# Small products of the first attention blocks on VectorE, and query spreads at every second unit, in a fused forward and backward kernel

## The chip, the cores and the metric

One core of one Trainium2 chip runs the whole program in one launch. The metric is the device time of that launch in microseconds (us). For this kernel about 0.3% (2.7 us) can be told from no change.

## The reference: what is computed

A gated mix of two branches, forward and backward. `A` is a causal sliding-window attention (2048 tokens, width 512, 32 heads of 16, window 256), `B` is a gated feed-forward net (512 to 1376 to 512). The kernel returns the output and the gradients of seven inputs.

```python
def _A_ref(x, wqkv, wo):
    qkv = (x @ wqkv).reshape(B, S, 3, H, Dh)  # q, k, v per head
    scores = einsum("bhqd,bhkd->bhqk", q, k) * (Dh ** -0.5)
    mask = (idx[:, None] - idx[None, :] >= 0) & (idx[:, None] - idx[None, :] < W)
    p = softmax(where(mask, scores, -1e9))
    return einsum("bhqk,bhkd->bhqd", p, v).reshape(B, S, D) @ wo
def _B_ref(x, W_gate, W_up, W_down):
    gate = x @ W_gate
    return ((gate * (gate > 0)) * (x @ W_up)) @ W_down
g = sigmoid((x * gate_w).sum(-1, keepdims=True))
out = g * _A_ref(x, wqkv, wo) + (1 - g) * _B_ref(x, W_gate, W_up, W_down)
# returned: out and the vjp of out for x, wqkv, wo, W_gate, W_up, W_down, gate_w
```

## The kernel before

The program has three stages. The feed-forward stage runs to about 245 us of the profiled span. The attention stage, forward and backward together, runs from there to about 712 us; the change lies in it. A last stage multiplies by the output weights and finishes the gradient of x.

**Units.** The 32 heads stand in four head groups of eight (`c` = 0 to 3) and the 2048 tokens in 16 blocks of 128 (`j` = 0 to 15). For every head group and query block the kernel goes through the key blocks of the window, each in two halves of four heads. One such piece, four heads of one query block against one key block, is a unit; there are 360. In the first head group block 0 has units U0 and U1, block 1 U2 to U5, block 2 U6 to U11, block 3 U12 to U17, block 4 U18 to U23, and so on, six to a block. A unit has a role: `d` (diagonal key block), `m` (the one before) or `f` (two before).

**What a unit does.** TensorE makes the scores `ST` (line 697), ScalarE their exponentials into `Pu` (L706), GpSimd masks them if the role is d or f (`affine_select`, L708 and L711), TensorE makes `dPT`, the products of the output gradient with v (L720), VectorE multiplies `Pd = Pu * dPT` (L725, called `gradp`; the tiles are named PPd, PPm or Pd by role), and TensorE sums over the keys into `BA` (L734 and L736, called `rowsum`). `ST` and `dPT` share four PSUM buffers, so a new one waits for an old one's reader. After the last unit of a block ScalarE copies `BA` to `BAs` (L740). `BA` has one buffer and `BAs` two: the first rowsum of the next block waits for the copy, and the copy of a block waits until the block two before it no longer uses its `BAs`.

**Small products.** `small_ops` (L768) then works on one block's `BAs`. `dve` (L780) takes the reciprocal of the row sums on VectorE. Four pieces follow on GpSimd: `pool1` (L783, L784, L786: the row term `ndel` and two products into `rq`), `pool2` (L789 into `rq`, L791 the attention output into `rows_st`), `pool3` (L794 and L795, a product and a sum in place in `BAs`), and `pool4` (L798, the gradient of q into `rows_st`). `pool4` is the last to read `BAs`. Each product is 128 partitions by 128 elements, with f32 inputs from SBUF, or bf16 for the rows.

**The order of the work** is written out by hand. A loop runs over step `n`, and step n issues the front of unit n, the `gradp` of unit n-2 and the `rowsum` of unit n-4 (`LAG` = 4). Events of a step hang in `ev`: GpSimd's events are issued after the front of the step (its mask included), VectorE's after the step's gradp. Every engine works through its own instructions in the order of issue. With s = n-2 at a block's last rowsum, the reciprocal stands at step s+3 and the four pieces at s+4, s+5, s+6, s+7; for block 0 of every head group at s+5, s+6, s+9, s+10. So in the first head group block 0 (s = 3) has its pieces at steps 8, 9, 12 and 13, block 1 (s = 7) at 11 to 14, block 2 (s = 13) at 17 to 20, block 3 (s = 19) at 23 to 26.

**Query spreads.** While four blocks are worked on, the projections of the next four are fed in between (`project_parts`): Q, dO, a transpose by DMA, K, V, and a transpose of K and V. Q and dO of eight heads lie in one tile `zT`; four copies on VectorE (`spread`, L125, 32 partitions by 1024 elements each) take them apart into the sparse tile `z` that the next blocks' `ST` and `dPT` read. The four are set when dO has been issued, at steps n+1, n+2, n+3 and n+4. The copies of K and V (L174, L196, L197) on VectorE follow when their projections are issued. There are 15 sets of four; the first is issued at once with its dO, before the attention loop, the other 14 by steps.

Of the kernel before, what the change touches and what calls it, by code (L numbers as in the profile page):

```python
# [9 lines left out]
ALU = mybir.AluOpType  # L10
# [12 lines left out]
def kernel(  # L23
# [20 lines left out]
    nc = tc.nc  # L44
# [8 lines left out]
    Dh = D // H  # L53
# [24 lines left out]
    def bc(ap2, n):  # L78
        return ap2.unsqueeze(2).to_broadcast([ap2.shape[0], ap2.shape[1], n])
# [37 lines left out]
    if True:  # L117
# [5 lines left out]
        def spread(gi, k):  # L123
            rows = slice(32 * k, 32 * k + 32)
            nc.vector.tensor_copy(zt[gi % ZB][rows, :, k, :, :].rearrange("p w t q -> p w (t q)"),  # L125
                                  proj[groups[gi]]["z"][rows, :, :])
# [76 lines left out]
    with ExitStack() as p1, tc.manual_schedule():  # L203
# [148 lines left out]
        for fc in range(FC):  # L352
            for tg in range(NTG):
                k = Step()
# [170 lines left out]
    if True:  # L525
# [242 lines left out]
        def small_ops(c, j, s):  # L768
            rows = proj[(c, j // TPG)]["rows"]
            jl = j % TPG  # L770
            rows_st = sts[c]
            BAs = BAsb[(c, j)]
            hd = lambda a: a.rearrange("p (h d) -> p h d", h=HG)
            rinv = wk.tile([P, HG], F32, tag="rinv", name="rinv")
            ndel = wk.tile([P, HG], F32, tag="ndel", name="ndel")
            rq = wk.tile([P, HG, 3 * Dh], BF, tag="rq", bufs=4, name="rq")
            RQ[(c, j)] = rq

            def dve():
                nc.vector.reciprocal(rinv[:], BAs[:, :, 16])  # L780

            def pool1():
                nc.gpsimd.tensor_tensor(out=ndel[:], in0=BAs[:, :, 33], in1=rinv[:], op=ALU.mult)  # L783
                nc.gpsimd.tensor_tensor(out=rq[:, :, 2 * Dh:3 * Dh], in0=hd(rows[:, 0, jl, :]),  # L784
                                        in1=bc(rinv[:], Dh), op=ALU.mult)
                nc.gpsimd.tensor_tensor(out=rq[:, :, 0:Dh], in0=rq[:, :, 2 * Dh:3 * Dh], in1=bc(ndel[:], Dh), op=ALU.mult)  # L786

            def pool2():
                nc.gpsimd.tensor_tensor(out=rq[:, :, Dh:2 * Dh], in0=hd(rows[:, 1, jl, :]),  # L789
                                        in1=bc(rinv[:], Dh), op=ALU.mult)  # L790
                nc.gpsimd.tensor_tensor(out=hd(rows_st[:, j, 3, :]), in0=BAs[:, :, 17:33], in1=bc(rinv[:], Dh), op=ALU.mult)  # L791

            def pool3():
                nc.gpsimd.tensor_tensor(out=BAs[:, :, 0:16], in0=BAs[:, :, 0:16], in1=bc(ndel[:], Dh), op=ALU.mult)  # L794
                nc.gpsimd.tensor_tensor(out=BAs[:, :, 0:16], in0=BAs[:, :, 0:16], in1=BAs[:, :, 34:50], op=ALU.add)  # L795

            def pool4():
                nc.gpsimd.tensor_tensor(out=hd(rows_st[:, j, 0, :]), in0=BAs[:, :, 0:16], in1=bc(rinv[:], Dh), op=ALU.mult)  # L798

            if c == DC - 1 and j > 8:  # L800
                return ((s + 3, "dve", dve), (s + 3, "pool+", pool1), (s + 4, "pool", pool2), (s + 6, "pool", pool3), (s + 7, "pool", pool4))
            at = (5, 6, 9, 10) if j == 0 else (4, 5, 6, 7)
            return ((s + 3, "dve", dve),) + tuple((s + a, "pool", f) for a, f in zip(at, (pool1, pool2, pool3, pool4)))

        GT = min(2, NT)
# [46 lines left out]
        with tc.manual_schedule():  # L852
            ev = {}
# [6 lines left out]
            n = 0  # L860
# [15 lines left out]
            def background():  # L876
                f, more = bgq.pop(0)
                store = f()
                if store is not None:
                    copies.append(store)  # L880
                    if len(copies) > 2 or gi + 2 >= len(groups):
                        ev.setdefault(n + 2, []).append(("dma", flush))
                return more
# [15 lines left out]
            while n <= NU + LAG or ev or cdq or bgq:  # L899
                now = ev.pop(n, [])  # L900
                u = units[n] if n < NU else None
                if u is not None:
                    gi = u.c * NTG + u.j // TPG
# [37 lines left out]
                if w is not None:  # L941
                    rowsum(w)
                    if not w.dma:
                        flip(w)
                    if w.last:
                        for s, eng, f in small_ops(w.c, w.j, n - 2):
                            ev.setdefault(s, []).append((eng, f))
                        done = [w.j - 2] if w.j >= 2 else []
                        if w.j == NT - 1:
                            done += [NT - 2, NT - 1]  # L950
                        for kb in done:
                            qbs = range(kb, min(NT, kb + 3))
                            for qb in qbs:
                                for half in range(2):
                                    e = n + (1 if qb < w.j else 5)
                                    cdq.append((e, w.c, kb, qb, half, qb == qbs[-1] and half == 1))
# [8 lines left out]
                if n >= NU:  # L965
                    if bgq:
                        held = background()
                    elif n > NU + 1:
                        for _ in range(2):
                            if len(S2["grads"]) > DC:  # L970
                                S2["grads"].pop(0)()
                elif held and credit > 0.3:
                    held = background()
                    credit -= 0.65
                elif prq and not held and ((credit > 0.4 and n > fed + 1) or due - n <= len(prq)):
                    fed = n
                    credit -= (0.44, 0.86, 0.86, 0.1, 0.86, 0.86)[len(prq) - 1]
                    prq.pop(0)()
                    if len(prq) == 4:
                        for k in range(NP):  # L980
                            ev.setdefault(n + 1 + k, []).append(("dve", lambda gi=gi, k=k: spread(gi + 1, k)))
                        ev.setdefault(n + 1, []).append(("dma", flush))
                    if not prq:
                        late += plan.get(gi + 1, [])
                elif bgq and len(prq) <= 2 and credit > 0.3:
                    held = background()
                    credit -= 0.65
# [28 lines left out]
    with ExitStack() as p56:  # L1016
        x_r5 = x_r

        with ExitStack() as p6, tc.manual_schedule():
# [43 lines left out]
            for g in range(NG):  # L1063
# [5 lines left out]
                for tl in range(GT):  # L1069
# [14 lines left out]
                    for c in range(DC):  # L1084
# [16 lines left out]
                                            op=ALU.mult)  # L1101
# [72 lines left out]
```

## Time and profile before

| | us |
|---|---|
| median of three runs | 902.75 (902.62, 902.75, 905.12) |
| the profiled execution | 903.0 |
| its span on the core | 901.3 |

The profiled execution lies 0.25 us above the median. Its span is 1.7 us shorter than its time. The granted TensorE clock was 1.0. VectorE was busy 511.1 us (57%), ScalarE 446.0 (49%), GpSimd 492.5 (55%). "Idle before" in a row of the timeline is the time for which the engine had nothing to run before the instruction, and the name behind the arrow is what ended it. A matmul's duration in a row is modelled and longer than the time after which the next one starts.

### The profile page before, as it was taken

The numbers are of one execution on the slowest core, as the hardware profiler recorded it, in microseconds if no ns is written. First come the engines' busy times: TensorE is split into PE (matmuls) and PEld (weight loads), VectorE is DVE, ScalarE is ACT, GpSimd is POOL, SyncE is SP. The second block draws the span as 40 slices with busy tenths as digits, with TensorE's granted clock in tenths as the row PEclk, the third lists the DMA queues.
The fourth block names the chain that finished last, engine by engine and source line by source line (L and its number), as shares of the span: only waits on it lengthen the run. The fifth ranks groups of instructions, "written<-read, shape, count | busy, mean of one in ns | idle before, by whom it ended". The sixth has DMA issues, their size and how long they took to land.

```text
span 901.3 us, 25949 instructions
## 1 busy us (share of the span) xinstructions
PE 889.4 (99%) x10607; PEld 560.3 (62%) x10607; DVE 511.1 (57%) x946; ACT 446.0 (49%) x787; POOL 492.5 (55%) x937
## 2 busy tenths in 40 slices
PE   9999999999999999999999999999999999999998
PEld 5555655655657777677776677766677544444445
DVE  4533334334468887678886788876787101333343
ACT  6422232222368778667776677766787112111111
POOL 4644545545277778667778567876788100222232
PEclk9999999999999999999999999999999999999999
DMA  9988989999999999998999989999999998998940
GB/s 299 204 182 195 197 178 209 214 230 201 202 144 159 196 183 190 194 169 153 175 187 179 190 162 176 192 193 184 209 190 195 225 259 219 252 277 234 198 125 30
DMA packets 520983, 174.57 MB, mean 194 GB/s; under 512 B 446816, under 2 KB 519744, under 8 KB 520864
## 3 DMA queue, kind: packets, MB, share of 16 engines
q1 hardware_dynamic: 498624, 150.62, 90.5%
q10 hardware_dynamic: 20608, 17.70, 7.0%
q0 software_dynamic: 1632, 4.59, 1.5%
q8 instruction: 83, 1.36, 0.6%
q14 instruction: 36, 0.29, 0.1%
HBM read 34.37 MB, written 36.24 MB: 78 GB/s over the span
## 4 chain that ended last, share of the span: by engine, by line
PE 87%; DVE 3%; SPq 3%; DMA 3%; ACT 2%; POOL 1%; issue 1%; DVEq 0%; POOLq 0%; ACTq 0%
PE wps L420 8%; PE ST L697 8%; PE dPT L720 8%; PE dxps L1076 7%; PE pt L763 5%; PE wps L651 5%; PE dhps L367 4%; PE CD L551 4%; PE BA L734 4%; PE ups L367 4%; PE gps L367 4%; PE pp L138 4%; PE dxps L1106 4%; PE dps L423 4%; PE bps L1051 3%; PE CD L554 3%
## 5 line engine op out<-in xcount | busy, mean ns | idle before, releaser
L697 PE MATMUL ST<-z,K 128*128 128x512 bf16 x360 | 136.0, 378 | 2.0 <-DVE PPm L725 1.2
L720 PE MATMUL dPT<-z,V 128*128 128x512 bf16 x360 | 135.9, 378 | 1.1 <-DVE Pd L725 0.5
L708 POOL TENSOR_SCALAR_AFFINE_SELECT PPd<-PPd 128x512 bf16<-128x512 bf16 x128 | 81.3, 636 | 77.9 <-ACT PPd L706 77.9
L381 POOL TENSOR_TENSOR hT<-rg,upm 128x512 bf16<-128x512 bf16 x44 | 51.0, 1159 | 113.1 <-DVE upm L379 98.5
L420 PE MATMUL wps<-dgu_r,x_r 128*128 128x256 bf16 (+1 forms) x704 | 101.8, 270 | 0.2 <-DVE wst L74 0.2
L725 DVE TENSOR_TENSOR PPd<-PPd,dPT 128x512 bf16<-128x512 bf16 x128 | 87.0, 680 | 19.3 <-PE dPT L720 12.6
L711 POOL TENSOR_SCALAR_AFFINE_SELECT Pu<-Pu 128x512 bf16<-128x512 bf16 x112 | 72.0, 643 | 34.9 <-ACT Pu L706 33.8
L706 ACT ACTIVATE PPd<-ST 128x512 bf16<-128x512 f32 x128 | 77.0, 603 | 23.8 <-PE ST L697 18.9
L725 DVE TENSOR_TENSOR Pd<-Pu,dPT 128x512 bf16<-128x512 bf16 x112 | 76.4, 682 | 20.6 <-PE dPT L720 10.0
L420 PEld LDWEIGHTS <-x_r 128*128 128x128 bf16 x704 | 68.0, 98 | 29.7 <-issue 0.5
L706 ACT ACTIVATE Pu<-ST 128x512 bf16<-128x512 f32 x112 | 67.4, 602 | 36.4 <-PE ST L697 36.3
L725 DVE TENSOR_TENSOR PPm<-PPm,dPT 128x512 bf16<-128x512 bf16 x120 | 80.1, 668 | 7.0 <-PE dPT L720 5.9
L706 ACT ACTIVATE PPm<-ST 128x512 bf16<-128x512 f32 x120 | 72.4, 604 | 16.4 <-PE ST L697 16.0
L379 DVE SCALAR_TENSOR_TENSOR upm<-rg,ups 128x512 bf16<-128x512 bf16 x44 | 30.2, 686 | 76.8 <-PE ups L367 53.0
L373 ACT ACTIVATE rg<-gps 128x512 bf16<-128x512 f32 x44 | 26.3, 597 | 83.7 <-PE gps L367 49.8
L1088 ACT COPY a_sb<-aps 128x512 f32<-128x512 f32 x16 | 9.4, 585 | 107.6 <-issue 100.1
L72 ACT COPY p<-pt 128x1024 bf16<-128x1024 bf16 x59 | 60.1, 1019 | 4.2
L391 POOL TENSOR_TENSOR dgu<-dh_sb,rg 128x512 bf16<-128x512 bf16 x44 | 57.8, 1314 | 5.3 <-ACT dh_sb L387 5.3
L423 PE MATMUL dps<-db_r,h_r 128*128 128x512 bf16 x160 | 60.6, 379 | 0.0
L390 DVE TENSOR_TENSOR dgu<-dh_sb,upm 128x512 bf16<-128x512 bf16 x44 | 33.2, 756 | 31.0 <-ACT dh_sb L387 27.2
L138 PE MATMUL pp<-x,p 128*128 128x512 bf16 x192 | 49.0, 378 | 0.0
L387 ACT CAST dh_sb<-dhps 128x512 bf16<-128x512 f32 x44 | 25.7, 585 | 41.1 <-PE dhps L367 41.0
(190 smaller groups left out, 2351.0 us busy)
## 6 DMA issues: line engine op xcount, KB each, us to landing
hT_d<-hT ACTq DMA_DIRECT2D x44, 128.0 KB, 2.5
dgT_d<-dgu ACTq DMA_DIRECT2D x44, 128.0 KB, 2.7
duT_d<-dgu ACTq DMA_DIRECT2D x44, 128.0 KB, 2.9
h<-hT_d SPq DMA_DIRECT2D x8, 640.0 KB, 5.4
dgT_g<-dgT_d SPq DMA_DIRECT2D x8, 640.0 KB, 5.8
duT_g<-duT_d SPq DMA_DIRECT2D x8, 640.0 KB, 6.4
dqkvo_d<-db_T SPq DMA_DIRECT2D x8, 512.0 KB, 4.2
go_g<-in_grad_out_dram SPq DMA_DIRECT2D x16, 256.0 KB, 4.6
```

The lines of the kernel that those rows point to most:

```text
L72: nc.scalar.copy(out, in_)
L138: nc.tensor.matmul(pp[:], lhsT=w_p[c][:, cd, which * P:(which + 1) * P], rhs=x_T[tg][:, cd, :], start=(cd == 0), stop=(cd == DC - 1))
L367: nc.tensor.matmul(out[:], lhsT=w(c), rhs=x(c), start=(c == 0), stop=(c == DC - 1))
L420: nc.tensor.matmul(acc["w"][:, c, 0:2 * nw], lhsT=x_r[:, t, c * P:(c + 1) * P], rhs=k.dgu_r[:, :, i, s0:P], start=(go_ and c % 2 == 0), st ...
L423: nc.tensor.matmul(acc["d"][:], lhsT=k.h_r[:, i, :], rhs=db_r[:, t, :], start=go_, stop=no_)
L697: nc.tensor.matmul(ST[:], lhsT=KTt[:, ksl], rhs=z[:, 0, :, jl, :], start=True, stop=True)
L706: nc.scalar.activation(u.Pu[:], ST[:], ACT.Exp)
L708: nc.gpsimd.affine_select(out=u.Pu[:], in_=u.Pu[:], compare_op=ALU.is_ge, fill=0.0, base=0, pattern=[[0, HH], [1, P]], channel_multiplier=-1)
L711: nc.gpsimd.affine_select(out=u.Pu[:], in_=u.Pu[:], compare_op=ALU.is_ge, fill=0.0, base=-1, pattern=[[0, HH], [-1, P]], channel_multiplier=1)
L720: nc.tensor.matmul(u.dPT[:], lhsT=VTt[:, ksl], rhs=z[:, 1, :, jl, :], start=True, stop=True)
L725: nc.vector.tensor_tensor(out=u.Pd[:], in0=u.Pu[:], in1=u.dPT[:], op=ALU.mult)
L1076: nc.tensor.matmul(to, lhsT=src[:, fc, lsl], rhs=W6[(wt, fc)][:, cols], start=(fc == 0 and wt == "Wg"), stop=False)
```

## The change

In the first head group the attention output (`rows_o`, L791) and the gradient of q (`pool4`) of blocks 0 to 3 go to VectorE, and in blocks 0 and 1 `pool3` too. Block 0 takes the same steps as the others (in the other head groups it keeps its later ones). The spreads of the 14 sets that go by steps stand at steps n+1, n+3, n+5 and n+7.

```diff
+            rows_eng = nc.vector if c == 0 and j < 4 else nc.gpsimd
+            sum_eng = nc.vector if c == 0 and j < 2 else nc.gpsimd
+
             def pool2():
                 nc.gpsimd.tensor_tensor(out=rq[:, :, Dh:2 * Dh], in0=hd(rows[:, 1, jl, :]),
                                         in1=bc(rinv[:], Dh), op=ALU.mult)
-                nc.gpsimd.tensor_tensor(out=hd(rows_st[:, j, 3, :]), in0=BAs[:, :, 17:33], in1=bc(rinv[:], Dh), op=ALU.mult)
+                if rows_eng is nc.gpsimd:
+                    rows_o()
+
+            def rows_o():
+                rows_eng.tensor_tensor(out=hd(rows_st[:, j, 3, :]), in0=BAs[:, :, 17:33], in1=bc(rinv[:], Dh), op=ALU.mult)
 
             def pool3():
-                nc.gpsimd.tensor_tensor(out=BAs[:, :, 0:16], in0=BAs[:, :, 0:16], in1=bc(ndel[:], Dh), op=ALU.mult)
-                nc.gpsimd.tensor_tensor(out=BAs[:, :, 0:16], in0=BAs[:, :, 0:16], in1=BAs[:, :, 34:50], op=ALU.add)
+                sum_eng.tensor_tensor(out=BAs[:, :, 0:16], in0=BAs[:, :, 0:16], in1=bc(ndel[:], Dh), op=ALU.mult)
+                sum_eng.tensor_tensor(out=BAs[:, :, 0:16], in0=BAs[:, :, 0:16], in1=BAs[:, :, 34:50], op=ALU.add)
 
             def pool4():
-                nc.gpsimd.tensor_tensor(out=hd(rows_st[:, j, 0, :]), in0=BAs[:, :, 0:16], in1=bc(rinv[:], Dh), op=ALU.mult)
+                rows_eng.tensor_tensor(out=hd(rows_st[:, j, 0, :]), in0=BAs[:, :, 0:16], in1=bc(rinv[:], Dh), op=ALU.mult)
 
             if c == DC - 1 and j > 8:
                 return (...)
+            if rows_eng is nc.vector:
+                return ((s + 3, "dve", dve), (s + 4, "pool", pool1), (s + 5, "pool", pool2), (s + 5, "dve", rows_o),
+                        (s + 6, "dve" if j < 2 else "pool", pool3), (s + 7, "dve", pool4))
             at = (5, 6, 9, 10) if j == 0 else (4, 5, 6, 7)
...
                         for k in range(NP):
-                            ev.setdefault(n + 1 + k, []).append(("dve", lambda gi=gi, k=k: spread(gi + 1, k)))
+                            ev.setdefault(n + 1 + 2 * k, []).append(("dve", lambda gi=gi, k=k: spread(gi + 1, k)))
                         ev.setdefault(n + 1, []).append(("dma", flush))
```

## The prediction, made before the changed kernel was built or run

> **What bounds the kernel now.** I read the page first: which engine is full, and which makes the chain that ended last.
>
> ```profile
> span 901.3 us, 25949 instructions
> PE 889.4 (99%) x10607; PEld 560.3 (62%) x10607; DVE 511.1 (57%) x946; ACT 446.0 (49%) x787; POOL 492.5 (55%) x937
> PE 87%; DVE 3%; SPq 3%; DMA 3%; ACT 2%; POOL 1%; issue 1%; DVEq 0%; POOLq 0%; ACTq 0%
> ```
>
> TensorE works 889.4 of 901.3 us and is 87% of the chain. The change leaves TensorE's work alone, so it gains only what TensorE now waits, and loses only where it makes TensorE wait. The list of TensorE's waits shows which can move:
>
> ```profile
> PE BA L734 <- ACT BAs L740: 1.8, 3, 1.2
> PE ST L697 <- DVE PPm L725: 1.2, 2, 0.6
> PE dPT L720 <- DVE Pd L725: 0.5, 1, 0.5
> PE ST L697 <- ACT PPm L706: 0.3, 1, 0.3
> PE dPT L720 <- DVE PPd L725: 0.2, 1, 0.2
> ```
>
> The longest is 1.2 us on `BAs`. The timelines of four engines place it in the first head group and follow it back.
>
> ```profile
> 263.91 0.18 PE L734 MATMUL BA<-KV,PPm 128*128 128x33 bf16 x1 [1.22 <-ACT BAs L740]
> 264.11 0.38 PE L697 MATMUL ST<-z,K 128*128 128x512 bf16 x1
> 264.33 0.18 PE L734 MATMUL BA<-KV,Pu 128*128 128x33 bf16 x1
> 261.25 0.60 ACT L706 ACTIVATE PPm<-ST 128x512 bf16<-128x512 f32 x1
> 263.37 0.49 ACT L740 COPY BAs<-BA 128x400 f32<-128x400 f32 x1 [1.53 <-POOL db_T L798]
> 260.76 0.40 POOL L794 TENSOR_TENSOR BAs<-BAs,ndel 128x128 f32<-128x128 f32 x1
> 262.94 0.40 POOL L798 TENSOR_TENSOR db_T<-BAs,rinv 128x128 bf16<-128x128 f32 x1
> 256.10 0.68 DVE L725 TENSOR_TENSOR PPm<-PPm,dPT 128x512 bf16<-128x512 bf16 x1
> 256.69 0.68 DVE L725 TENSOR_TENSOR Pd<-Pu,dPT 128x512 bf16<-128x512 bf16 x1
> 257.89 0.20 DVE L780 RECIPROCAL rinv<-BAs 128x8 f32<-128x8 f32 x1
> 258.00 0.64 DVE L725 TENSOR_TENSOR PPm<-PPm,dPT 128x512 bf16<-128x512 bf16 x1
> 263.00 0.69 DVE L725 TENSOR_TENSOR Pd<-Pu,dPT 128x512 bf16<-128x512 bf16 x1 [1.85 <-POOL Pu L711]
> core 0: us, PE busy (x) PEld busy (x) DVE busy (x) ACT busy (x) POOL busy (x), PEclk, DMA share, GB/s
> 256.00:264.00 8.00, 6.31 (x100) 4.19 (x99) 5.55 (x11) 6.19 (x12) 7.43 (x19) 1.00 1.22 188
> ```
>
> Block 3's first rowsum (U12, at 263.91) waits for the copy of block 2's `BAs`, and this for block 0's `pool4` (L798, 262.94): `BAs` has two buffers, and block 0's pieces stand late. GpSimd is behind: 7.43 us busy of 8.00 from 256 to 264. VectorE has 2.45 us free there, 1.85 of them waiting for GpSimd's mask of U13.
>
> **The change, part 1: blocks 0 and 1.** Eight products leave GpSimd for VectorE: L791, L794, L795 and L798 of two blocks. Block 0's `pool4` moves from step 13 on GpSimd to step 10 on VectorE, behind the gradp of U8 (step n holds the gradp of unit n-2). The copy of `BAs` could then start behind the exponential of U15 (261.25 + 0.60), and the 1.22 us go. A matmul's row is longer than the time to the next start (at 264.11 0.38, but the next starts 0.22 later), so such an idle time is really up to 0.16 more; I count 1.4. The 0.2 for PPd is of the same backlog and too small to count.
>
> What is late next is VectorE's own list. No row shows such a product on VectorE. Near rows:
>
> ```profile
> L1096 DVE TENSOR_TENSOR amb<-a_sb,b_all 128x512 f32<-128x512 f32 x16 | 11.0, 685 | 0.0
> L1102 DVE TENSOR_TENSOR dz<-dz 128x1 f32<-128x1 f32 x16 | 2.5, 159 | 0.6
> L125 DVE COPY z<-zT x60: 405/520/890, 243.9 to 651.5; 32x1024 bf16<-32x1024 bf16 x60
> L390 DVE TENSOR_TENSOR dgu<-dh_sb,upm x44: 411/775/1394, 20.9 to 234.2; 128x512 bf16<-128x512 bf16 x44
> 121.52 0.78 DVE L390 TENSOR_TENSOR dgu<-dh_sb,upm 128x512 bf16<-128x512 bf16 x1 [0.73 <-ACT dh_sb L387]
> 120.86 1.15 POOL L381 TENSOR_TENSOR hT<-rg,upm 128x512 bf16<-128x512 bf16 x1 [2.76 <-DVE upm L379]
> 259.16 0.63 POOL L711 TENSOR_SCALAR_AFFINE_SELECT Pu<-Pu 128x512 bf16<-128x512 bf16 x1
> ```
>
> Between 128x1 (159 ns) and 128x512 in f32 (685) a 128x128 product comes to 159 + 127 x 526/511 = 290 ns. Gradps of 0.68 follow each other every 0.60 (256.10, 256.69), so 0.08 overlaps and a product adds 0.21 to the list. That is the lower bound. The upper comes from L390, which also has two inputs in SBUF: 411 ns at best, 775 in the middle. The one at 121.52 lasts until 122.30, 0.29 after GpSimd's L381 ends at 122.01; it seems to wait that product out. If each product waits out a mask of 0.63, it adds 0.84.
>
> The Trainium skill states this as a rule (SBUF — State Buffer, Who interferes with whom): a VectorE instruction with two SBUF inputs contends with a GpSimd instruction that reads SBUF, and the one that comes second fully blocks. By that rule the trace's L390 agrees (0.78 beside GpSimd, 0.41 alone), and the rule speaks against this change, as GpSimd keeps masking all the while.
>
> I take 0.37: 0.21 and a mean wait of 0.16, which is what the 60 spreads show, beside the same GpSimd work (mean 564 against 405 at best; x60 in 33.8 us). Eight make 2.96. VectorE's list from 256.10 to the gradp of U13 is then seven gradps at 0.60, a reciprocal of 0.11 (257.89 to 258.00) and 2.96: U13 starts at 256.10 + 4.20 + 0.11 + 2.96 = 263.37 and ends at 264.06, against 263.69 before. Its rowsum, 264.33 before, can follow at 264.08: **0.25 gained of 1.4**. At 0.21 the gradp ends at 262.78 and all 1.4 is gained; at 0.84 it ends at 267.8, a loss of 3.5. Queued behind each product are the gradps of U7 to U13, and for each waits its rowsum. `pool3` on VectorE also waits for GpSimd's `ndel`, made two steps before, so nothing is counted for that. Block 0's earlier steps cost GpSimd nothing: it loses eight products of 0.40.
>
> **Part 2: blocks 2 and 3.** Four more products go to VectorE, at steps 18, 20, 24 and 26. Block 2's two fall into time VectorE spends waiting for the projections of Q and dO (0.68 and 0.85 idle); block 3's two fall among spreads and copies of K and V.
>
> ```profile
> 267.44 0.69 DVE L152 TENSOR_SCALAR zT<-pp 128x512 bf16<-128x512 f32 x1 [0.68 <-PE pp L138]
> 270.17 0.69 DVE L74 CAST zT<-pp 128x512 bf16<-128x512 f32 x1 [0.85 <-PE pp L141]
> 281.11 0.68 DVE L725 TENSOR_TENSOR PPm<-PPm,dPT 128x512 bf16<-128x512 bf16 x1
> 282.53 0.18 PE L734 MATMUL BA<-KV,PPm 128*128 128x33 bf16 x1
> ```
>
> The tightest unit behind them is U27: gradp ends at 281.79, its rowsum starts at 282.53, 0.74 later. Block 3's products take 2 x 0.37 = 0.74 of that, and TensorE wants it 0.25 earlier: **0.25 lost**, between 0 (0.21 each) and 1.2 (0.84 each). With part 1 the head group is even.
>
> **Part 3: the spreads.** Their number stays; two of a set's four move behind gradps that were behind them. It pays where TensorE waits on a gradp right after a set:
>
> ```profile
> 472.14 0.89 DVE L125 COPY z<-zT 32x1024 bf16<-32x1024 bf16 x1
> 473.84 0.42 DVE L125 COPY z<-zT 32x1024 bf16<-32x1024 bf16 x1
> 474.29 0.69 DVE L725 TENSOR_TENSOR PPm<-PPm,dPT 128x512 bf16<-128x512 bf16 x1
> 475.04 0.38 PE L697 MATMUL ST<-z,K 128*128 128x512 bf16 x1 [0.60 <-DVE PPm L725]
> 590.93 0.38 PE L697 MATMUL ST<-z,K 128*128 128x512 bf16 x1 [0.60 <-DVE PPm L725]
> 621.63 0.38 PE L720 MATMUL dPT<-z,V 128*128 128x512 bf16 x1 [0.53 <-DVE Pd L725]
> 306.23 0.68 DVE L174 TENSOR_SCALAR V<-VT,par 128x512 bf16<-128x512 bf16 x2 [0.85 <-ACT VT L72]
> ```
>
> At 475.04 and 590.93 three copies stand before the gradp that TensorE awaits, afterwards two: 0.42 to 0.89 less, against a wait of 0.60 + 0.16. I take 0.70 each. At 621.63 two copies go behind the gradp, and the whole 0.53 + 0.16 goes. Together 2.1. In the other sets VectorE runs without a pause from the dO cast to beyond the K and V copies, so its end stays where it was: nothing. One set can lose: where VectorE idled for V (0.85 at 306.23), all four copies were done ahead of the idle time; now one stands behind it and delays what follows by up to one copy (0.56). I take 0.3. Part 3: **1.8 gained**, between -0.6 (only that loss, one copy) and 2.2 (all three waits, no loss).
>
> **Sum.** 0.25 - 0.25 + 1.8 = 1.8 us. The profiled execution goes from 903.0 to 901.2, its span from 901.3 to 899.5; it lies 0.25 above the median, so the median goes from 902.75 to 901.0 (0.2%).
>
> **The rivals.**
>
> *Faster: VectorE has room for all of it.* The products cost 0.21, part 1 gives 1.4 and part 2 nothing; the spreads give 2.2. Then 902.75 - 3.6 = 899.1. For it: VectorE's 2.45 us free from 256 to 264, and that GpSimd, relieved, stops making gradps wait (1.85 at 263.00). Against it: the copies of 0.89 in the same trace.
>
> *Slower: the products wait for GpSimd each time.* At 0.84 each VectorE's list reaches U13's gradp 4.1 us later than now: part 1 loses 3.5, part 2 1.2, and with the spreads' 1.8 the time is 902.75 + 2.9 = 905.7. It decides from about 0.6 a product, where part 1 alone loses more than the spreads give. By the skill's rule the wait is at most what is left of a running instruction; a mask under way is met on average at its half (0.32), which makes 0.53. That speaks for a loss inside the head group, and against the whole of this price.
>
> *No change: the copies only move the wait.* VectorE's list up to the sixth gradp after dO is as long as before, so a wait removed at 475 returns some gradps later, and the spreads give nothing: 902.75 less 0.25 plus 0.25, 902.75. For it: VectorE's list is dense behind every set. Against it: the waits listed stand right at the sets.
>
> **Chances.** The forecast (gain of 0.5 to 2.7) 0.46; faster 0.33; no change 0.11; slower 0.10. The parts' bounds and the three cases give 898.6 to 904.0. By 0.3% (2.7 us) faster 0.33, the same 0.57, slower 0.10.
>
> **What would show it.** Right: no 1.2 us wait on `BAs` near 263; block 0's L798 on VectorE near 259; the rows of L791, L794 and L798 on VectorE at a mean near 0.45 (0.29 alone); TensorE's waits at 475, 591 and 621 gone; new short waits of TensorE on gradps between 258 and 264. Wrong: products of 0.7 and more, a wait on gradps above 1 us in the first head group, or new waits behind the later sets.

## The result, and the profile after

The changed kernel takes 906.54 us in the median of 20 runs, the kernel before beside it 903.88. The ratio is 1.0029, with an interval of [1.0017, 1.0041]: slower by 0.3%, against a forecast of 0.2% faster, and 2.5 us above the top of the range. (The kernel before itself stands 1.1 us higher in these 20 runs than in the three known to the forecast; the changed kernel lies outside the range without that too.)

The profiled execution is the fastest of the twenty (903.46), so its span says nothing against the span of before. The loss is seen inside it. Page of the changed kernel, span and engines:

```profile
span 901.7 us, 25949 instructions
PE 888.8 (99%) x10607; PEld 561.2 (62%) x10607; DVE 510.6 (57%) x958; ACT 445.7 (49%) x787; POOL 490.1 (54%) x925
```

Twelve instructions went from GpSimd (937 before) to VectorE (946 before). TensorE's work is the same, as forecast. Its list of waits, changed kernel, whole span (us in total, times, longest):

```profile
PE ST L697 <- ACT PPm L706: 2.5, 7, 0.4
PE pt L763 <- DVE p L74: 2.0, 6, 0.4
...
PE ST L697 <- DVE PPm L725: 0.6, 1, 0.6
...
PE dPT L720 <- DVE Pd L725: 0.2, 1, 0.2
```

The wait on `BAs` (1.2) is gone, the two waits of 0.6 on PPm at 475 and 591 are gone, and that at 621 is 0.2. In their place stand 2.5 us of `ST` behind an exponential (0.3 before) and 2.0 us of `pt`, TensorE's transposes (L763), behind a copy of `p` by VectorE. The line of `pt` was in no list of before.

To place the loss I use one instruction that each unit has, its `ST`. From the first (U0) to that of U312, early in the last head group, in the timelines of TensorE, kernel before and then changed kernel:

```profile
245.51 0.38 PE L697 MATMUL ST<-z,K 128*128 128x512 bf16 x1
641.19 0.38 PE L697 MATMUL ST<-z,K 128*128 128x512 bf16 x1
```

```profile
245.15 0.38 PE L697 MATMUL ST<-z,K 128*128 128x512 bf16 x1
643.76 0.38 PE L697 MATMUL ST<-z,K 128*128 128x512 bf16 x1
```

395.68 us before, 398.61 after: 2.9 us lost. The difference of the medians is 2.7, and 2.9 lies within the interval of the ratio. The table shows how far the changed kernel stands behind the kernel before at the `ST` of several units, both counted from U0, read in this way from the traces.

| at unit | 18 | 42 | 66 | 108 | 132 | 156 | 180 | 198 | 222 | 246 | 270 | 288 | 312 |
|---|---|---|---|---|---|---|---|---|---|---|---|---|---|
| us behind | 0.19 | 0.22 | 1.06 | 1.30 | 1.30 | 2.06 | 2.81 | 2.28 | 2.29 | 3.03 | 3.79 | 3.26 | 2.94 |

The head of the stage, where the products moved, costs 0.2. Five stretches of 24 units cost about 0.75 to 0.84 each (42 to 66, 132 to 156, 156 to 180, 222 to 246, 246 to 270). Three gain: 0.53 before U198, 0.53 before U288, 0.32 before U312; these are the three that the forecast counted on.

**The head.** VectorE in the changed kernel, timeline, with two of GpSimd's masks; behind it the row of busy time from 256 to 264:

```profile
256.33 0.60 DVE L798 TENSOR_TENSOR db_T<-BAs,rinv 128x128 bf16<-128x128 f32 x1
257.46 0.28 DVE L801 TENSOR_TENSOR BAs<-BAs,ndel 128x128 f32<-128x128 f32 x1
257.77 0.61 DVE L802 TENSOR_TENSOR BAs<-BAs 128x128 f32<-128x128 f32 x1
258.89 0.54 DVE L805 TENSOR_TENSOR db_T<-BAs,rinv 128x128 bf16<-128x128 f32 x1
263.17 0.28 DVE L805 TENSOR_TENSOR db_T<-BAs,rinv 128x128 bf16<-128x128 f32 x1
263.37 0.67 DVE L725 TENSOR_TENSOR Pd<-Pu,dPT 128x512 bf16<-128x512 bf16 x1
256.10 0.69 POOL L708 TENSOR_SCALAR_AFFINE_SELECT PPd<-PPd 128x512 bf16<-128x512 bf16 x1
258.65 0.63 POOL L711 TENSOR_SCALAR_AFFINE_SELECT Pu<-Pu 128x512 bf16<-128x512 bf16 x1 [0.42 <-ACT Pu L706]
```

```profile
256.00:264.00 8.00, 6.61 (x97) 4.00 (x94) 7.93 (x18) 6.33 (x11) 5.47 (x14) 1.00 1.23 195
```

VectorE (third engine in the row) is busy 7.93 of 8.00 us there, 5.55 before; GpSimd 5.47, 7.43 before. Block 0's `pool4` (now L805) stands at 258.89 instead of 262.94, and no copy of `BAs` waits for it. The longest waits that replace it are for PSUM buffers that two gradps free, those of U9 and U12:

```profile
260.15 0.38 PE L697 MATMUL ST<-z,K 128*128 128x512 bf16 x1 [0.56 <-DVE PPm L725]
263.30 0.38 PE L720 MATMUL dPT<-z,V 128*128 128x512 bf16 x1 [0.29 <-DVE PPm L725]
```

**A set that loses.** VectorE in the stretch from U132, changed kernel (the same work of before is in the fence behind it, with ScalarE's rows that bring K and V):

```profile
418.21 0.69 DVE L725 TENSOR_TENSOR PPd<-PPd,dPT 128x512 bf16<-128x512 bf16 x1
419.76 0.62 DVE L174 TENSOR_SCALAR K<-KT,par 128x512 bf16<-128x512 bf16 x2 [0.87 <-ACT KT L72]
421.00 0.58 DVE L125 COPY z<-zT 32x1024 bf16<-32x1024 bf16 x1
422.58 0.65 DVE L174 TENSOR_SCALAR V<-VT,par 128x512 bf16<-128x512 bf16 x2 [0.27 <-ACT VT L72]
423.15 0.68 DVE L725 TENSOR_TENSOR Pd<-Pu,dPT 128x512 bf16<-128x512 bf16 x1
423.86 0.42 DVE L125 COPY z<-zT 32x1024 bf16<-32x1024 bf16 x1
424.31 0.69 DVE L74 COPY p<-pt 128x1024 bf16<-128x1024 bf16 x1
```

```profile
419.00 0.52 DVE L125 COPY z<-zT 32x1024 bf16<-32x1024 bf16 x1
419.54 1.03 DVE L174 TENSOR_SCALAR K<-KT,par 128x512 bf16<-128x512 bf16 x2
421.74 0.62 DVE L174 TENSOR_SCALAR V<-VT,par 128x512 bf16<-128x512 bf16 x2
422.27 0.68 DVE L725 TENSOR_TENSOR Pd<-Pu,dPT 128x512 bf16<-128x512 bf16 x1
422.87 0.69 DVE L74 COPY p<-pt 128x1024 bf16<-128x1024 bf16 x1
418.20 0.58 ACT L72 CAST KT<-pp 128x512 bf16<-128x512 f32 x1 [0.55 <-PE pp L138]
421.12 0.59 ACT L72 CAST VT<-pp 128x512 bf16<-128x512 f32 x1 [0.51 <-PE pp L138]
```

Before, K is there at 418.78, but VectorE is in the spreads until 419.52 and takes K up 0.74 late; V it takes up as it arrives (421.71), and nothing is idle. Now VectorE idles 0.87 for K and 0.27 for V, does the third spread after K, and the fourth (423.86) after V and directly ahead of the copy of `p`. That copy empties a PSUM buffer that TensorE needs for its next transposes. It starts 1.16 after the start of the gradp before it, against 0.60 before. TensorE in the changed kernel:

```profile
425.05 0.38 PE L763 MATMUL pt<-ident,Pu 128*128 128x128 bf16 x4 [0.33 <-DVE p L74]
427.31 0.38 PE L697 MATMUL ST<-z,K 128*128 128x512 bf16 x1 [0.42 <-ACT PPm L706]
```

and ScalarE, whose own copy of the following `pt` then comes late (its idle time in the bracket), with the exponential behind it that `ST` at 427.31 waits for:

```profile
425.75 1.01 ACT L72 COPY p<-pt 128x1024 bf16<-128x1024 bf16 x1 [0.58 <-PE pt L763]
426.66 0.60 ACT L706 ACTIVATE PPm<-ST 128x512 bf16<-128x512 f32 x1
```

### The profile page after: what moved, and what is told of

It is laid out like the page before. It is cut to its first block, busy times and chain, and to the rows that moved or that the text cites. A ratio compares the mean times of both kernels' runs of the same rounds, so it can differ in the third digit from the quotient of the medians.

```text
span 901.7 us, 25949 instructions
## 1 busy us (share of the span) xinstructions
PE 888.8 (99%) x10607; PEld 561.2 (62%) x10607; DVE 510.6 (57%) x958; ACT 445.7 (49%) x787; POOL 490.1 (54%) x925
## 3 DMA queue, kind: packets, MB, share of 16 engines
q8 instruction: 83, 1.36, 0.6%
## 4 chain that ended last, share of the span: by engine, by line
PE 94%; DVE 2%; ACT 2%; issue 1%; DMA 1%; SPq 0%; POOL 0%; DVEq 0%; ACTq 0%
PE wps L420 8%; PE dPT L720 8%; PE dxps L1086 8%; PE ST L697 8%; PE pt L763 6%; PE pp L138 5%; PE wps L651 5%; PE dxps L1116 4%; PE CD L551 4%; PE BA L734 4%; PE dhps L367 4%; PE bps L1061 4%; PE ups L367 4%; PE gps L367 4%; PE dps L423 4%; PE CD L554 3%
```

## The experiments

All are compared with the kernel before. "At U312" is the time from the `ST` of U0 to that of U312, against 395.68 us of before; "at U18" and "at U42" likewise. Runs with a ratio were also timed; the others are one profiled execution each. In the edits `...` stands for the rest of a line or for lines left out.

| run | at U18 | at U42 | at U312 | time against before |
|---|---|---|---|---|
| the change | +0.19 | +0.22 | +2.94 | 1.0029 [1.0017, 1.0041] |
| spreads only | +0.01 | +0.09 | +2.83 | 1.0029 [1.0014, 1.0045] |
| products only | +0.19 | +0.69 | +0.71 | 0.9999 [0.9986, 1.0012] |
| kernel before again | +0.01 | +0.01 | +0.05 | |
| spreads at 1, 3, 4, 6 | 0.00 | -0.11 | -1.11 | 0.9995 [0.9981, 1.0009] |
| spreads at 1, 3, 5, 6 | +0.01 | -0.10 | -0.55 | |
| spreads at 1, 3, 4, 7 | +0.01 | +0.05 | +2.51 | |
| last spread behind `p` | +0.01 | +0.09 | +0.81 | |
| block 0 early, on GpSimd | -0.71 | -0.71 | -0.71 | |
| products of blocks 0 and 1 | +0.19 | +0.19 | +0.22 | |
| both small changes | -0.72 | -0.83 | -2.25 | 0.9985 [0.9971, 0.9999] |

### Which half of the change makes the loss

The spreads alone:

```diff
-ev.setdefault(n + 1 + k, [])...
+ev.setdefault(n + 1 + 2 * k, [])...
```

> The kernel before with the spreads at n+1, n+3, n+5, n+7 and nothing else; the products stay on GpSimd. The attention stage from the first ST to the last took 448.64 us before and 450.73 after the change. Theory A (the spreads made the loss: a copy at n+7 stands ahead of the copy of p that TensorE's transposes wait for, and the waits for K and V are no longer filled): the stage takes 450.5 (+1.9 against before), with the six waits pt <- p of about 0.4 in the trace, and the time is 0.2% longer than before. Theory B (the products made the loss and the spreads gain, as predicted): the stage takes 446.8 (-1.8), no such waits.

The products alone, in the changed kernel:

```diff
-ev.setdefault(n + 1 + 2 * k, [])...
+ev.setdefault(n + 1 + k, [])...
```

> The changed kernel with the spreads back at n+1 to n+4; products on VectorE and block 0's earlier steps stay. Theory A (the spreads made the loss): the stage from the first ST to the last takes 448.8 (+0.2 against before), no waits pt <- p, and the time is the same as before within 0.1%. Theory B (the products made it): 450.5 or more (+1.9), waits of TensorE on gradps in the first head group above 2 us in sum.

And the kernel before, unchanged:

> The kernel before, unchanged, once more, to see how far the stage times repeat from one execution to another. If the attention stage repeats, it takes 448.6 within 0.2 again, while the stage before it and the one after it may differ by more; if it does not repeat, differences of 2 us between two traces mean nothing.

Theory A holds. The spreads alone lose 2.83 us at U312 with six waits `pt` on `p`, and their ratio is that of the whole change. The products alone leave the time where it was. The two parts, 2.83 and 0.71, make 3.54, more than the 2.94 of both: between U18 and U42 the products of blocks 2 and 3 cost 0.50 with the old spreads and nothing with the new (0.18 of products at U18, 0.13 at U42: the change less the spreads only).

The kernel before repeats within 0.05 us up to U312. Behind it, it does not: its last `ST` comes 1.50 earlier than in the first trace. So the whole stage, in which these expectations were put (447.1 for the kernel before again, 450.6 for the spreads, 447.8 for the products), cannot carry differences of 1.5 us, and I read no trace beyond U312. Up to there three further runs repeat as well: those whose edits lie in the first blocks alone (products only, products of blocks 0 and 1, block 0 early) keep their distance from the kernel before within 0.04 us from U42 to U312.

### What in the spreads loses

Other steps, for the kernel before:

```diff
-ev.setdefault(n + 1 + k, [])...
+ev.setdefault(n + (1, 3, 4, 6)[k], [])...
```

> The kernel before with the spreads at n+1, n+3, n+4, n+6: two and not three ahead of the gradp that TensorE waited for, one in VectorE's wait for K, one in its wait for V, none at n+7. Theory A: the waits at 475, 591 and 621 go (together up to 2.1), those behind the K and V copies do not grow, no pt <- p: the stage takes 446.6 (-2.0), the time is 0.2% shorter. Theory C (any copy that leaves the first four steps comes back as a wait behind the K and V copies): 448.6 or more.

At U312 it is 1.11 ahead, about half of what was expected, and the time cannot be told from before (0.9995, the interval holds 1). By sets: 0.47 gained before U198, 0.46 before U288, 0.42 before U312, and 0.11 (U18 to U42) and 0.08 (U66 to U90) in the first head group; but 0.09 lost between U42 and U66 and 0.26 between U90 and U108, and next to nothing elsewhere. Theory C, that any copy that leaves the first four steps comes back, falls at U312; by the whole stage (448.4) nothing can be said.

Two things differ between these steps and the change's: a copy stands in VectorE's wait for K, and none at n+7. One at a time (`(1, 3, 5, 6)[k]` and `(1, 3, 4, 7)[k]` in the same line):

> The kernel before with the spreads at n+1, n+3, n+5, n+6: the last copy is no longer at n+7, but none is at n+4, where VectorE waits for K. Read at ST of U312, where two runs of the kernel before agreed within 0.05 us, spreads at n+1, n+3, n+5, n+7 stood 2.83 us behind the kernel before and n+1, n+3, n+4, n+6 1.11 ahead. Theory A1 (it is the copy at n+7, ahead of the copy of p): no waits pt <- p, U312 0.5 to 1.1 ahead. Theory A2 (it is VectorE's wait for K that no copy fills any more): 2 to 3 behind, as with the last at n+7.

> The kernel before with the spreads at n+1, n+3, n+4, n+7: the wait for K is filled, the last copy is at n+7 again. Theory A1 (the copy at n+7): U312 2 to 3 us behind the kernel before, with the waits pt <- p of 0.3 and more. Theory A2 (the unfilled wait for K): 0.5 to 1.1 ahead, no such waits. If both are needed, both runs stand near the kernel before.

With the last copy at n+6 the kernel is 0.55 ahead; with the wait for K filled and the last at n+7 it is 2.51 behind, with the waits of the change again (list of waits of that run, 245 to 712 us):

```profile
PE ST L697 <- ACT PPm L706: 2.5, 7, 0.4
PE pt L763 <- DVE p L74: 1.9, 6, 0.4
```

So the copy at n+7 is the cause (A1). The unfilled wait for K (A2) is a small part: 0.56 with the last copy at n+6 (1.11 against 0.55 ahead), 0.32 with it at n+7 (2.83 against 2.51 behind). What about it, its order against the copy of `p` or its lateness? The last spread at the end of the same step:

```diff
-ev.setdefault(n + 1 + k, []).append(("dve", ...))
+ev.setdefault(n + 1 + 2 * k, []).append(("dma" if k == 3 else "dve", ...))
```

("dma" events are issued last in a step.)

> The kernel before with the spreads at n+1, n+3, n+5 and n+7, but the last one issued at the end of its step, behind the copy of p. If the order of these two instructions makes the loss, the waits pt <- p go and U312 stands near the run with the last at n+6 (0.55 ahead of the kernel before; 0.3 behind to 1 ahead). If it is the lateness of the last copy as such, U312 is 2 to 3 us behind.

Neither expectation is met: 0.81 behind. The waits `pt` on `p` are gone, and with them 2.02 of the 2.83; that is the price of the order of two instructions. The rest stays, the waits of `ST` on PPm among it (2.0 in six waits); what holds up those exponentials was not followed. From there to the copy at n+6 (0.55 ahead) are another 1.36. At n+6 the copy falls into time in which VectorE waits for V. In the run with the steps 1, 3, 4, 6 the wait is still 0.49 long behind it:

```profile
420.56 0.48 DVE L125 COPY z<-zT 32x1024 bf16<-32x1024 bf16 x1
421.54 0.78 DVE L174 TENSOR_SCALAR V<-VT,par 128x512 bf16<-128x512 bf16 x2 [0.49 <-ACT VT L72]
```

### What the products cost

The products of blocks 0 and 1 alone (`rows_eng` for `j < 2`, spreads as before):

> The products of blocks 0 and 1 alone on VectorE, with block 0's earlier steps; blocks 2 and 3 on GpSimd, spreads as before. With blocks 0 to 3 U18 stood 0.19 us behind the kernel before and U42 0.69. If the products of blocks 2 and 3 cost the 0.5 between the two, U18 stays at 0.2 behind and U42 is 0.2 behind as well; if blocks 0 and 1 leave VectorE late in the first set of spreads, U42 stays near 0.7 behind.

U42 stays at 0.19: the products of blocks 2 and 3 cost the other 0.50 beside the old spreads. And block 0's earlier steps without any product on VectorE:

```diff
-at = (5, 6, 9, 10) if j == 0 else (4, 5, 6, 7)
+at = (5, 6, 9, 10) if j == 0 and c > 0 else (4, 5, 6, 7)
```

> The kernel before with block 0 of the first head group at steps s+4 to s+7, all on GpSimd: no product on VectorE, spreads as before. Theory D (it is block 0's late steps, not GpSimd's load, that make TensorE wait 1.2 us on BAs): that wait goes and U18 stands 0.5 to 1.2 us ahead of the kernel before. Theory E (GpSimd is too full for the earlier steps, its masks come later): new waits on gradps behind the masks, U18 between 0.3 ahead and 1 behind.

Theory D holds: 0.71 gained by the steps alone. GpSimd has the room: block 0's `pool4` in that run, then the copy of block 2's `BAs` on ScalarE, which follows the exponential without a wait:

```profile
260.77 0.40 POOL L798 TENSOR_TENSOR db_T<-BAs,rinv 128x128 bf16<-128x128 f32 x1
```

```profile
263.17 0.60 ACT L706 ACTIVATE PPm<-ST 128x512 bf16<-128x512 f32 x1 [0.36 <-PE ST L697]
263.66 0.49 ACT L740 COPY BAs<-BA 128x400 f32<-128x400 f32 x1
```

Against the change's 0.19 behind, the products on VectorE cost 0.90 in these two blocks.

### Both small changes together

Block 0's earlier steps on GpSimd, no product on VectorE, and 1, 3, 4, 6 for the spreads only in the sets where that run gained (the other sets at 1, 2, 3, 4):

```diff
-at = (5, 6, 9, 10) if j == 0 else (4, 5, 6, 7)
+at = (5, 6, 9, 10) if j == 0 and c > 0 else (4, 5, 6, 7)
...
-ev.setdefault(n + 1 + k, [])...
+at = (1, 3, 4, 6)[k] if gi in (1, 3, 8, 12, 13) else 1 + k
+ev.setdefault(n + at, [])...
```

> The kernel before with block 0 of the first head group at the others' steps on GpSimd, and the spreads at n+1, n+3, n+4, n+6 in the sets fed during blocks 4 to 7 and 12 to 15 of the first head group, blocks 0 to 3 of the third, and blocks 0 to 7 of the fourth; all other sets as before. If the two gains add up, U312 stands 0.71 + 1.54 = 2.25 us ahead of the kernel before and the time is 0.25% shorter; if the sets depend on each other, 0.7 to 1.5 ahead.

2.25 ahead at U312, as the sum had it, and 0.9985 [0.9971, 0.9999] in time: 900.92 us in the median beside 902.29 of the kernel before. In the traces this is ahead of both kernels; in time the gain of 0.15% is small, and its interval only just leaves out 1.

## Why the prediction was wrong

**Bounds.** Right: TensorE's work did not change (889.4 and 888.8 us busy), and what the losing sets lost is in its waits.

**Part 1, blocks 0 and 1.** The wait on `BAs` went, and the list of VectorE became the limit, as forecast; a price a little too low and the place where TensorE feels the list were wrong. Mean durations of the four products in the changed kernel:

```profile
L805 DVE TENSOR_TENSOR db_T<-BAs,rinv 128x128 bf16<-128x128 f32 x4 | 1.9, 469 | 0.5 <-POOL BAs L802 0.5
L798 DVE TENSOR_TENSOR db_T<-BAs,rinv 128x128 bf16<-128x128 f32 x4 | 1.5, 364 | 0.0
L802 DVE TENSOR_TENSOR BAs<-BAs 128x128 f32<-128x128 f32 x2 | 1.2, 604 | 0.1
L801 DVE TENSOR_TENSOR BAs<-BAs,ndel 128x128 f32<-128x128 f32 x2 | 0.9, 436 | 0.0
```

Together 5.5 us for twelve, 0.46 each, where 0.45 was forecast. The gradp of U13 was to start at 263.37; it does, in a trace whose first `ST` is 0.36 earlier, so 0.36 late. The list has no idle time there: from 255.74 the seven gradps and the reciprocal take 4.24 and the eight products 3.39, 0.42 each where 0.37 was counted. Nor does TensorE wait at the rowsum of U13, by which the forecast read the gain. It waits earlier, for the PSUM buffers that the gradps of U9 and U12 free: 0.56 at 260.15 and 0.29 at 263.30, for which nothing was added. The 0.25 gained became 0.19 lost. With two waits of about 0.3 on exponentials, TensorE's waits up to U18 add up to 1.39, against 1.68 before. They alone would be a gain of 0.29, so 0.48 stands in no such row and stays open.

**The price.** 0.28 us is a product alone (263.17, with GpSimd idle); 0.60 the one at 256.33, which began beside a GpSimd mask. That mask ends at 256.79 and the product 0.14 later; the product at 258.89 ends 0.15 after its mask. Of the eight, the five that began beside a mask took 0.54 to 0.61 and end 0.13 to 0.15 after it, and the other three took 0.28. By the Trainium skill (SBUF — State Buffer, Who interferes with whom), the second of the two to come waits for the whole of the first; these rows agree with it. The products took neither the lower nor the upper price: a mask is waited for only as far as it still has to run, and the rival in which each product waits out a whole mask (0.84) did not come. The forecast took its mean wait from the spreads, another instruction; that it came within 0.05 is not shown to be more than luck.

**Part 2, blocks 2 and 3.** 0.25 lost was forecast. It was 0.50 with the spreads as they were and nothing with the new ones, so the direction was right for the old spreads, and in the change the term does not count.

**Part 3, the spreads.** This is where the prediction failed. The three waits shrank in the direction forecast, by two thirds of the size: 1.38 gained (0.53, 0.53, 0.32) of 2.1. The first two gave a little less than the 0.60 that their rows show, so the 0.16 added to each did not appear; of the third 0.21 stayed. The step that failed is this sentence: "In the other sets VectorE runs without a pause from the dO cast to beyond the K and V copies, so its end stays where it was: nothing." The end did not stay. What stands behind a spread at n+7 is not the next gradp but, in some sets, the copy of `p`, issued in the same step behind VectorE's events. The forecast left this instruction out of the queue. In each of the four sets that lose 0.75, TensorE waits 0.33 for that copy and 0.42 for the exponential behind it (425.05 and 427.31), together the whole loss. The order of the two instructions alone is worth 2.02 us over all sets.

The pause is the smaller part. The trace of before showed none in these sets because the third and fourth spread stood ahead of K's copies and held them up (for 0.74 in the set at U132). Moved, they leave 0.87 and 0.27 of pause, and the work behind ends later. The set fed from U66 to U90 has the same pauses without a wait on `p`, and loses 0.24. With the steps 1, 3, 5, 6 the pause for K is as long in the set at U132 (0.87), and that set loses 0.10. Changed kernel, then spreads at 1, 3, 5, 6:

```profile
332.00 0.62 DVE L174 TENSOR_SCALAR K<-KT,par 128x512 bf16<-128x512 bf16 x2 [0.87 <-ACT KT L72]
```

```profile
419.88 0.62 DVE L174 TENSOR_SCALAR K<-KT,par 128x512 bf16<-128x512 bf16 x2 [0.87 <-ACT KT L72]
```

One set was seen to idle for V, and 0.3 counted for it; it lost 0.84 (U42 to U66), with a wait on `p` of 0.39 in it. This sign chose the wrong sets. In the trace of before four more sets idle for V, against the sentence quoted, and none of them loses:

```profile
396.32 0.64 DVE L174 TENSOR_SCALAR V<-VT,par 128x512 bf16<-128x512 bf16 x2 [2.41 <-ACT VT L72]
```

The other three are at 361.85 (0.85), 512.23 and 628.82 (2.41 each). In sum the spreads' share is 0.84 + 0.24 + 4 x 0.75 - 1.38 = 2.7, in place of a gain of 1.8.

**The range.** The bounds of the three parts add up to a loss of 5.3 (908.0 us); the range ended at 904.0 and left even its own slower rival (905.7) outside.

**The rivals.** The slower rival's time (905.7) is the nearest to the one measured, by luck: its mechanism, products that each wait out a mask, did not come. "No change" came nearest in kind (a wait removed returns some gradps later), but held that VectorE's list stays as long as before, which is the same mistake, and left out the copy of `p` as well. "Block 0's late steps alone" was no rival, and is the gain that was there: 0.71 without any product moved.

**What would have shown it before.** The trace of before has 0.22 between the end of the copy of `p` at 422.87 and the transposes that use its buffer next:

```profile
423.78 0.38 PE L763 MATMUL pt<-ident,Pu 128*128 128x128 bf16 x4
```

422.87 + 0.69 = 423.56; a copy of 0.42 ahead of it cannot be hidden in 0.22. I read the slack of gradps and not that of this copy.

## What to carry to other kernels

A queue without pauses does not show that its order is free: some of its work stands in time that would be idle, and moved out of it, makes the list longer. What it is moved in front of can cost more than the pause. Before work is moved behind later instructions, find what each of them releases (here a PSUM buffer for transposes), and its slack, not only that of the instructions that the move is to help. And where a buffer is held by late work, try the earlier step on the same engine before another engine; here that gained 0.71 where the move to another engine lost 0.19.

## What the runs showed of the hardware

Spread out, the copies ran shorter: VectorE's 60 spreads took 564 ns in the mean before and 483 after, and the copies of K 473 and 382. The run with the spreads alone has the same (486 and 386), so it is not the relief of GpSimd. Groups by line, kernel before and then changed kernel:

```profile
L125 DVE COPY z<-zT 32x1024 bf16<-32x1024 bf16 x60 | 33.8, 564 | 1.5
L174 DVE TENSOR_SCALAR K<-KT,par 128x512 bf16<-128x512 bf16 x32 | 13.9, 473 | 2.2 <-ACT KT L72 1.9
```

```profile
L125 DVE COPY z<-zT 32x1024 bf16<-32x1024 bf16 x60 | 29.0, 483 | 1.5
L174 DVE TENSOR_SCALAR K<-KT,par 128x512 bf16<-128x512 bf16 x32 | 10.9, 382 | 13.8 <-ACT KT L72 13.8
```

That is 4.8 and 3.0 us less of VectorE's time, in the same change that made the kernel slower. The time did not shorten the list: VectorE idled 13.8 us ahead of K's copies, where it was 2.2.

Up to U312 two executions of one program agreed within 0.05 us in 395.68; from there to the last `ST` they differed by 1.5. What makes the last 48 units vary was not tried and stays open.
